# Decode attention with a gated FFN: K and V loaded head by head into adjacent partitions, FFN weights moved in the queue, a new tail

## The chip, the cores and the metric

One NeuronCore of a Trainium2 chip. The metric is device time in microseconds, the median of several executions. "Span" is the length of the profiled execution on the core, about 2 us less than its device time. A run is called slow here if it lies more than 1.5% above the fastest run of its kernel; ratios use the others ("fast") only.

PE is the matrix engine, DVE, ACT and POOL are the vector, scalar and general-purpose engines, and SP issues most of the loads; a "q" behind a name is its instruction queue. SBUF is the on-chip memory that loads fill, in 128 rows called partitions; products go to PSUM. FFN is the feed-forward network. The page is the printed summary of one profiled execution. A load is called landed at the last increment of its semaphore in the trace (16 increments for one load of K or V).

## The reference, cut to what matters

One decode step for two batches: layer norm, attention of 16 query heads over 8 K/V heads in a window of the last 2048 positions, then a gate from a small FFN.

```python
B, D = 2, 448; Hq, Hkv, Sk, Dh = 16, 8, 8192, 256; W = 2048; Dff = 1792
xn = layernorm(x)
q = xn @ wq                                      # wq: 448 x 4096
p = softmax(q . k_cache[:, :, Sk-W:, :] / 16)    # K, V: 2 x 8 x 8192 x 256, bf16
s = (p . v_cache[:, :, Sk-W:, :]) @ wo           # wo: 4096 x 448
g = silu(relu(xn @ w1) @ w2)                     # w1: 448 x 1792, w2: 1792 x 448
out = x + s * g
```

Each byte of the windows of K and V (33.6 MB), of wq and wo (3.7 MB each), and of w1 and w2 (1.6 MB each) is read once: 44.1 MB. Hardly anything is computed per byte.

## The kernel before

K and V are cut into four units of four heads, 4 MB for each of K and V. One unit's K goes through: transposes on PE, copies out of PSUM, scores, softmax. Its V is then multiplied. Loads are issued by the SP queue, in the order K0, wq, K1, V0, K2, V1, K3, V2, w1, w2, V3, wo, as buffers come free.

```python
def kv_src(u, cache):                    # partition = 4 * r + head, 32 KB of one head's rows each
    b, v = divmod(u, 2)
    return cache[b, 4*v:4*v+4, SK-W:SK, :].rearrange("h (r t) d -> r h (t d)", t=NT)   # NT = 64

def load_k(u):                           # one load of 128 partitions
    d_k[u] = pr.dma(SP, kbuf[u % 2][:, :], kv_src(u, A_k_cache), [st.get(("T", u - 2))])
# ... (cut)
# tail, after the softmax of unit 3:
do_H(); attend_turn(2); do_hT(); do_F(); do_PV(3); attend_scale(3); attend_turn(3)
# ... (cut: two products and two copies spread the attention output over partitions)
for j in range(32):                      # wo: four column groups of PE at once
    for i in range(4):
        lo = j * D + i * NCOL            # NCOL = 112
        m_o = pr.op(PE, mm(obk[32*i:32*i+B, 0:NCOL], at2[:, 2*j:2*j+2], wo_sb[:, lo:lo+NCOL],
                           j == 0, j == 31, tile_position=(0, 32*i)), deps)
# ... (cut) out = wo result * g + x, then one output DMA per batch, from SP and from ACT
```

Of the kernel before, what the change touches and what calls it, by code (L numbers as in the profile page):

```python
# [14 lines left out]
class _Op:  # L15
    __slots__ = ("eng", "fn", "deps", "dma", "needed", "value", "sem")

    def __init__(self, eng, fn, deps, dma):
        self.eng, self.fn, self.deps, self.dma = eng, fn, deps, dma
        self.needed, self.value, self.sem = dma, 0, None  # L20


class _Prog:
# [11 lines left out]
    def dma(self, eng, dst, src, deps=()):  # L35
        o = _Op(eng, lambda e: e.dma_start(dst, src), [d for d in deps if d is not None], True)  # L36
        self.lists[eng].append(o)
        return o

    def run(self, block):  # L40
        n = 0
# [4 lines left out]
        for e, ops in self.lists.items():  # L46
            sem, count = self.es.enter_context(self.nc.semaphore(f"s_{e}")), 0
            for o in ops:
                if o.dma:
                    n += 1  # L50
                    o.sem, o.value = self.es.enter_context(self.nc.semaphore(f"d_{n}")), 16
                elif o.needed:
                    count += 1
                    o.sem, o.value = sem, count

        def emit(eng, ops):
            seen = {}
            for o in ops:
# [9 lines left out]
                if o.needed:  # L68
                    made.then_inc(o.sem, 16 if o.dma else 1)
# [7 lines left out]
def bass_recurrent_scan__sliding_block_cached__dense_activation_relu__decode_kernel(  # L77
# [28 lines left out]
    WO_PARTS = [12, 12, 4, 2, 2]  # L106
    NCOL = D // 4
    NTB = 5
# [5 lines left out]
    with es:  # L114
# [17 lines left out]
        qmask = named("qmask", [128, 4], F32)  # L132
        own = named("own", [128, 4], F32)
        far = named("far", [128, 4], F32)
        low = named("low", [128, 4], F32)
        fold = named("fold", [128, 32], BF)
        fold8 = named("fold8", [128, 8], F32)
# [11 lines left out]
        h_sb = named("h_sb", [128, 28], BF)  # L149
        x_c = named("x_c", [128, NCOL], BF)  # L150
        ea = named("ea", [128, NCOL], F32)
        g_sb = named("g_sb", [128, NCOL], F32)
        tmp = named("tmp", [128, NCOL], F32)
        out_sb = named("out_sb", [128, NCOL], BF)
# [12 lines left out]
        at_exp = named("at_exp", [128, 256], BF)  # L167
        at2 = named("at2", [128, 64], BF)
# [13 lines left out]
        def kv_src(u, cache):  # L182
            b, v = divmod(u, 2)
            return cache[b, 4 * v:4 * v + 4, SK - W:SK, :].rearrange("h (r t) d -> r h (t d)", t=NT)

        d_x = pr.dma(ACTE, x_sb[0:B, :], A_x[:, 0, :])
        p_xc = pr.op(POOL, lambda e: e.memset(x_c[:, :], 0.0))
        d_xc = [pr.dma(ACTE, view(x_c, 0, [[1, NCOL]], n=4, p0=b, pstep=32),
                       A_x[b, 0, :].rearrange("(i n) -> i n", i=4), [p_xc]) for b in range(B)]

        wq_sb, w1_sb, w2_sb, wo_sb = vbuf[1], kbuf[0], kbuf[0], kbuf[1]
# [4 lines left out]
        wo_src = A_wo.rearrange("(p j) n -> p (j n)", j=32)  # L196
# [4 lines left out]
        def load_k(u):  # L201
            d_k[u] = pr.dma(SP, kbuf[u % 2][:, :], kv_src(u, A_k_cache), [st.get(("T", u - 2))])

        def load_v(u, cuts=(0, NT)):
            deps = [None if u == 0 else st["q_mm"] if u == 1 else st["PV", u - 2]]
            d_v[u] = []
            for lo, hi in zip(cuts, cuts[1:]):
                d_v[u].append((hi, pr.dma(SP, vbuf[u % 2][:, lo * DH:hi * DH],
                                          kv_src(u, A_v_cache)[:, :, lo * DH:hi * DH], deps)))
# [4 lines left out]
        load_v(0)  # L214

# [9 lines left out]
        p_qz = pr.op(POOL, lambda e: e.memset(qz[:, :], 0.0), [p_one])  # L225

# [9 lines left out]
        for e2 in range(2):  # L236
# [10 lines left out]
            out=qmask[:, :], in_=view(ident, 0, [[32, 4], [1, 32]]), axis=AX.X, op=ALU.add))  # L247

        def fold_op(e):
            with nc.allow_low_precision("zeros and ones"):  # L250
                return e.tensor_reduce(out=fold[:, :], in_=view(ident, 0, [[1, 32], [32, 4]]), axis=AX.X, op=ALU.add)
        v_fold = pr.op(DVE, fold_op)
        v_f8 = pr.op(DVE, lambda e: e.tensor_reduce(
# [5 lines left out]
        v_low = pr.op(DVE, lambda e: e.tensor_scalar(  # L259
            out=low[:, :], in0=own[:, :], scalar1=1.0, scalar2=-LOW, op0=ALU.subtract, op1=ALU.mult), [v_own])  # L260
# [49 lines left out]
        def softmax(u, fill=()):  # L310
            fill = list(fill)

            def meanwhile():
# [5 lines left out]
                out=rm4[:, :], in_=view(sbk, 0, [[1, 4], [4, 128]]), axis=AX.X, op=ALU.max), [st["S", u]])  # L319
# [16 lines left out]
                out=view(s_sb, 0, [[4, 128], [1, 4]]), in0=view(sbk, 0, [[4, 128], [1, 4]]), scalar=bias[:, 0:1],  # L336
                in1=view(low, 0, [[0, 128], [1, 4]]), op0=ALU.add, op1=ALU.min),
# [19 lines left out]

        def do_PV(u, gs=range(4)):
            bank, src, p = obk, vbuf[u % 2], pt[u % 2]
            for g in gs:  # L360
                deps = [next(d for hi, d in d_v[u] if hi >= 16 * g + 16), st["pt", u], a_z, st["obk"]]
# [9 lines left out]
        def attend_scale(u):  # L371
            st["osb", u] = st["obk"] = pr.op(DVE, lambda e: e.tensor_scalar(  # L372
                out=o_sb[:, :], in0=obk[:, :], scalar1=rs[:, u:u + 1], scalar2=None, op0=ALU.mult),
                [st["PV", u], st["rs", u], st.get(("oT", u - 1))])

        def attend_turn(u):
            b, v = divmod(u, 2)
            deps = [st["osb", u], v_fold, st["mbk"]]
            for dhi in range(2):
# [6 lines left out]
                out=view(at_exp, 128 * b + 64 * v, [[8, 8], [4, 2], [1, 4]]),  # L386
                in0=view(mbk, 136, [[1, 8], [8, 2], [0, 4]]),
                in1=view(qmask, 0, [[0, 8], [0, 2], [1, 4]]), op=ALU.mult), [o, v_qm])
# [35 lines left out]
        def do_hT():  # L424
            hbk = tb[0][:, :].bitcast(F32).tensor
            deps = [st["h_n"], evac[NU * NCHUNK - 4]]
            for j in range(7):
# [4 lines left out]
            st["hT"] = pr.op(DVE, lambda e: e.tensor_copy(  # L432
                view(h_sb, 0, [[2, 7], [14, 2], [1, 2]]), view(hbk, 0, [[4, 7], [2, 2], [1, 2]])), [o])

        def do_F():
            fbk = tb[1][:, :].bitcast(F32).tensor
            deps = [st["w2"], st["hT"], evac[NU * NCHUNK - 3]]
            for f in range(14):
                for i in range(4):
                    lo = W2_AT + f * D + i * NCOL  # L440
                    o = pr.op(PE, mm(view(fbk, 0, [[1, NCOL]], n=B, p0=32 * i), h_sb[:, 2 * f:2 * f + 2], w2_sb[:, lo:lo + NCOL],
# [109 lines left out]
```

## Time and profile before

| | before |
|---|---|
| device time, median | 112.91 us (112.71 to 113.01) |
| span | 110.9 us |
| read from HBM | 44.1 MB |
| landing of one 4 MB unit after the other (last engine of K1 to last of V2, 5 units) | 9.75 us |
| one 32 KB packet, median | 1213 ns |
| last landing of wo; end | 107.46; 110.9 us |

Packet times and landings of single engines come from the trace's packet and semaphore records. Lines from the page of the kernel before: busy tenths of the 16 DMA engines in 40 slices; the DMA queue (packets, MB, share of 16 engines' time); what was read; and the chain of work that ended last, by engine and by line.

```profile
span 110.9 us, 1921 instructions
...
DMA  3988979898899889889989998998999999999920
...
q1 hardware_dynamic: 2584, 44.11, 93.5%
...
HBM read 44.11 MB, written 0.00 MB: 398 GB/s over the span
...
DMA 56%; PE 34%; DVE 4%; SPq 2%; issue 1%; ACT 1%
```

Those engines are busy nearly everywhere. In this table of one stretch of the kernel before, the last two figures are the DMA share and GB/s:

```profile
core 0: us, PE busy (x) PEld busy (x) DVE busy (x) ACT busy (x) POOL busy (x), PEclk, DMA share, GB/s
30.00:70.00 40.00, 33.59 (x285) 22.04 (x284) 20.91 (x43) 15.90 (x20) 0.00 (x0) 0.83 1.00 431
```

At 431 GB/s, 44.1 MB take 102.3 us. The DMA issues of the kernel before (count, KB of one, median us from issue to landing) show one DMA per unit:

```profile
kbuf<-in_A_k_cache_dram SPq DMA_DIRECT2D x4, 4096.0 KB, 27.1
vbuf<-in_A_v_cache_dram SPq DMA_DIRECT2D x3, 4096.0 KB, 37.0
...
out_dram<-out_sb SPq DMA_DIRECT2D x1, 0.9 KB
out_dram<-out_sb ACTq DMA_DIRECT2D x1, 0.9 KB
```

And how often PE waits for K (total us, times, longest), and the end of the chain of waits (start, us, what):

```profile
PE tb L285 <- DMA kbuf<-in_A_k_cache_dram: 6.3, 2, 5.4
```

```profile
83.07 24.39 DMA kbuf<-in_A_wo_dram
107.46 0.04 issue
107.50 0.39 PE obk L265 x8
107.91 0.28 DVE tmp L513
108.22 0.27 DVE out_sb L515
```

The kernel ends when the last slice of wo has landed, plus 3.4 us. It is bound by the DMA stream.

### The profile page before, as it was taken

The page shows a single profiled execution, that of the slowest core. Times are in us where ns is not written, and L with a number is a line of the kernel's source. Part 1 is how long each engine was busy: PE and PEld are TensorE (multiplying, and loading weights), DVE is VectorE, ACT ScalarE, POOL GpSimd, SP SyncE. Part 2 cuts the span into 40 slices and gives each one's busy share as a digit, 9 for nine tenths or more (in the row PEclk, how much of TensorE's full clock was granted, in tenths as well). Part 3 has the DMA queues.
Part 4 walks back from the last instruction along what each step waited for, and adds up shares of the span by engine and source line. Part 5 has one row for each costly group of instructions (what it writes and reads, how often), then busy time and mean ns, then how long its engine had stood idle before and what let it go on. Part 6 is the DMA issues. An engine that isn't in the chain of part 4 may idle for free.

```text
span 110.9 us, 1921 instructions
## 1 busy us (share of the span) xinstructions
PE 74.0 (67%) x845; PEld 49.7 (45%) x845; DVE 48.0 (43%) x110; ACT 35.4 (32%) x43; POOL 1.9 (2%) x11
## 2 busy tenths in 40 slices
PE   0010299995428999859999949699985464293480
PEld 0000299952127977413777513397632244022350
DVE  2182042953433356553775653477546333104001
ACT  1960036760020647602286602076820200000000
POOL 6000000000000000000000000000000000000000
PEclk9999999999995589995899995799999985555555
DMA  3988979898899889889989998998999999999920
GB/s 95 473 379 379 520 331 496 355 567 372 378 532 414 378 378 556 384 378 532 417 366 390 526 402 378 520 426 378 387 382 416 454 434 423 408 426 427 394 98 1
DMA packets 2619, 44.22 MB, mean 399 GB/s; under 512 B 306, under 2 KB 564, under 8 KB 948
## 3 DMA queue, kind: packets, MB, share of 16 engines
q1 hardware_dynamic: 2584, 44.11, 93.5%
q8 instruction: 6, 0.10, 0.3%
q10 hardware_dynamic: 28, 0.00, 0.0%
q14 instruction: 1, 0.01, 0.0%
HBM read 44.11 MB, written 0.00 MB: 398 GB/s over the span
## 4 chain that ended last, share of the span: by engine, by line
DMA 56%; PE 34%; DVE 4%; SPq 2%; issue 1%; ACT 1%
DMA kbuf<-in_A_k_cache_dram 34%; PE tb L285 25%; DMA kbuf<-in_A_wo_dram 22%; PE sbk L265 5%; PE obk L265 2%; SPq L36 2%; PE mbk L265 1%; DVE s_sb L335 1%; ACT e_sb L340 1%; DVE rm L318 1%; DVE q_n L399 1%; PE mbk L345 1%; DVE pt L350 0%; DVE qz L409 0%; PE mbk L403 0%
## 5 line engine op out<-in xcount | busy, mean ns | idle before, releaser
L285 PE MATMUL tb<-ident_f,kbuf 128*128 128x128 f32 x256 | 36.6, 306 | 6.3 <-DMA kbuf<-in_A_k_cache_dram 6.3
L285 PEld LDWEIGHTS tb<-ident_f,kbuf 128*128 128x128 f32 x256 | 33.5, 161 | 10.4 <-DMA kbuf<-in_A_k_cache_dram 6.4
L295 ACT ACTIVATE kt<-tb 128x1024 bf16<-128x1024 bf16 x28 | 27.4, 1023 | 26.2 <-PE tb L285 26.2
L293 DVE COPY kt<-tb 128x1024 bf16<-128x1024 bf16 x36 | 24.7, 690 | 21.7 <-PE tb L285 21.7
L265 PE MATMUL obk<-vbuf,pt 128*16 128x512 bf16 x128 | 13.5, 529 | 3.5 <-DMA vbuf<-in_A_v_cache_dram 3.5
L265 PE MATMUL sbk<-kt,qz 128*32 128x512 bf16 x128 | 11.0, 393 | 1.7 <-DVE kt L293 1.1
L340 ACT ACTIVATE e_sb<-s_sb 128x512 bf16<-128x512 f32 x4 | 2.5, 630 | 22.9 <-DVE s_sb L335 22.9
L265 PEld LDWEIGHTS obk<-vbuf,pt 128*16 128x16 bf16 x128 | 3.2, 101 | 8.2 <-DMA vbuf<-in_A_v_cache_dram 4.4
L265 PE MATMUL mbk<-ident,xg 2*128 2x2 bf16 x7 | 0.3, 163 | 7.4 <-DVE xg L237 7.4
L372 DVE TENSOR_SCALAR o_sb<-obk,rs 128x512 bf16<-128x512 f32 x4 | 2.9, 735 | 5.4 <-PE obk L265 5.4
L265 PEld LDWEIGHTS sbk<-kt,qz 128*32 128x32 bf16 x128 | 2.7, 94 | 5.5 <-DVE kt L293 2.1
L265 PE MATMUL obk<-kbuf,at 128*2 128x112 bf16 x128 | 3.7, 292 | 2.1 <-DMA kbuf<-in_A_wo_dram 1.8
L318 DVE TENSOR_REDUCE rm<-sbk 128x4 f32<-128x512 f32 x4 | 2.8, 691 | 4.3 <-PE sbk L265 4.3
L350 DVE COPY pt<-mbk 128x512 bf16<-128x512 bf16 x4 | 1.7, 424 | 5.6 <-PE mbk L345 5.6
L345 PE MATMUL mbk<-ident,e_sb 128*128 128x128 bf16 x16 | 2.2, 286 | 2.6 <-ACT e_sb L340 2.6
L265 PEld LDWEIGHTS obk<-kbuf,at 128*2 128x2 bf16 x128 | 2.6, 112 | 3.1 <-DMA kbuf<-in_A_wo_dram 2.6
L265 PEld LDWEIGHTS mbk<-ident,xg 2*128 2x128 bf16 x7 | 0.3, 101 | 7.4 <-DVE xg L237 7.4
L345 PEld LDWEIGHTS mbk<-ident,e_sb 128*128 128x128 bf16 x16 | 1.3, 122 | 5.0 <-ACT e_sb L340 5.0
L323 PE MATMUL mbk<-ident_f,rm 128*1 128x128 f32 x4 | 1.1, 270 | 3.4 <-DVE rm L321 3.4
L265 PE MATMUL mbk<-one_f,mall 1*128 1x1 f32 x8 | 1.6, 268 | 2.5 <-DVE mall L330 2.5
L335 DVE SCALAR_TENSOR_TENSOR s_sb<-sbk,bias,low 128x512 f32<-128x512 f32 x4 | 3.0, 751 | 0.1
L323 PEld LDWEIGHTS mbk<-ident_f,rm 128*1 128x1 f32 x4 | 0.3, 79 | 5.4 <-DVE rm L321 5.4
(68 smaller groups left out, 37.0 us busy)
## 6 DMA issues: line engine op xcount, KB each, us to landing
kbuf<-in_A_k_cache_dram SPq DMA_DIRECT2D x4, 4096.0 KB, 27.1
vbuf<-in_A_v_cache_dram SPq DMA_DIRECT2D x3, 4096.0 KB, 37.0
vbuf<-in_A_wq_dram SPq DMA_DIRECT2D x1, 3584.0 KB, 20.1
kbuf<-in_B_w_dram SPq DMA_DIRECT2D x2, 1568.0 KB, 23.6
vbuf<-in_A_v_cache_dram SPq DMA_DIRECT2D x1, 3072.0 KB, 25.8
kbuf<-in_A_wo_dram SPq DMA_DIRECT2D x2, 1344.0 KB, 22.2
vbuf<-in_A_v_cache_dram SPq DMA_DIRECT2D x1, 1024.0 KB, 27.7
kbuf<-in_A_wo_dram SPq DMA_DIRECT2D x1, 448.0 KB, 24.3
```

The lines of the kernel that those rows point to most:

```text
L36: o = _Op(eng, lambda e: e.dma_start(dst, src), [d for d in deps if d is not None], True)
L265: return lambda e: e.matmul(out_ap, lhsT=lhsT, rhs=rhs, start=start, stop=stop, skip_group_check=True, **kw)
L285: o = pr.op(PE, lambda e, n=n, lo=lo: e.matmul(bank_f[:, n * 128:(n + 1) * 128], lhsT=src_f[:, lo:lo + 128], rhs=ident_f[:, :], start=True ...
L293: evac[n_th] = pr.op(DVE, lambda e: e.tensor_copy(dst[:, :], bank[:, :]), deps)
L295: evac[n_th] = pr.op(ACTE, lambda e: e.activation(dst[:, :], bank[:, :], ACT.Copy), deps)
L318: v = pr.op(DVE, lambda e: e.tensor_reduce(out=rm4[:, :], in_=view(sbk, 0, [[1, 4], [4, 128]]), axis=AX.X, op=ALU.max), [st["S", u]])
L323: m = st["rmT", u] = pr.op(PE, lambda e: e.matmul(mbk_ap(0, 128, 1), lhsT=rm[:, :], rhs=ident_f[:, :], start=True, stop=True, is_transpose ...
L335: v = st["shift", u] = pr.op(DVE, lambda e: e.scalar_tensor_tensor(out=view(s_sb, 0, [[4, 128], [1, 4]]), in0=view(sbk, 0, [[4, 128], [1, ...
L340: a = st["exp", u] = pr.op(ACTE, lambda e: e.activation(e_sb[:, :], s_sb[:, :], ACT.Exp, accum_out=ssum[:, 0:1]), [v, st.get(("Pt", u - 1) ...
L345: o = pr.op(PE, lambda e, j=j: e.matmul(mb16[:, 512 + 128 * j:640 + 128 * j], lhsT=e_sb[:, 128 * j:128 * j + 128], rhs=ident[:, :], start= ...
L350: v = st["pt", u] = pr.op(DVE, lambda e: e.tensor_copy(view(pt[u % 2], 0, [[256, 2], [16, 16], [8, 2], [1, 8]]), view(mb16, 512, [[256, 2] ...
L372: st["osb", u] = st["obk"] = pr.op(DVE, lambda e: e.tensor_scalar(out=o_sb[:, :], in0=obk[:, :], scalar1=rs[:, u:u + 1], scalar2=None, op0 ...
```

## The change

Its parts: each head of a unit gets its own plain load into 32 adjacent partitions (four loads per unit); w1 and w2 move up in the queue to between V0 and K2, into their own buffer, and the FFN is computed there; wo is read in two halves by head group, into K2's buffer, so that it no longer waits for K3; the wo and FFN products place each of the eight output rows (batch and quarter of the columns) in adjacent partitions, by shifted zero-padded weights, so that one output DMA does; a few idle products (`idle_work` in the code) are added on PE; I took them to be there for the PE clock, which the code does not say.

```diff
-            return cache[b, 4 * v:4 * v + 4, SK - W:SK, :].rearrange("h (r t) d -> r h (t d)", t=NT)
+            return cache[b, 4 * v:4 * v + 4, SK - W:SK, :].rearrange("h (r t) d -> h r (t d)", t=NT)
+
+        def kv_pairs(u, cache, buf, lo=0, hi=UW):
+            src = kv_src(u, cache)
+            return [(buf[32 * h:32 * h + 32, lo:hi], src[h, :, lo:hi]) for h in range(4)]
...
-            d_k[u] = pr.dma(SP, kbuf[u % 2][:, :], kv_src(u, A_k_cache), [st.get(("T", u - 2))])
+            d_k[u] = pr.dmas(SP, kv_pairs(u, A_k_cache, kbuf[u % 2]), [st.get(("T", u - 2))])
... (V alike; dmas issues a list of DMAs on one semaphore; the score masks follow the new partition order)
         load_v(0)
+        st["w1"] = pr.dma(SP, w1_sb[:, 0:W2_AT], w1_src)
+        st["w2"] = pr.dma(SP, ..., w2_src)
...
         attend_scale(0)
+        do_H()
+        do_hT()
+        do_F()
...
-    WO_PARTS = [12, 12, 4, 2, 2]
+    WO_PARTS = [8, 8, 6, 4, 4, 2]
-        wo_src = A_wo.rearrange("(p j) n -> p (j n)", j=32)
+        wo_src = A_wo.rearrange("(v p j) n -> v p (j n)", v=2, j=NWO)
...
-        do_H()
+        idle_work(3)
+        do_PV(3, (0,))
         attend_turn(2)
... (cut: the rest of unit 3's V products, spreads, idle products)
-                m_o = pr.op(PE, mm(obk[32 * i:32 * i + B, 0:NCOL], at2[:, 2 * j:2 * j + 2], wo_sb[:, lo:lo + NCOL],
-                                   j == 0, j == 31, tile_position=(0, 32 * i)), deps)
+                m_o = pr.op(PE, mm(obk[0:NROW, 0:NCOL], at_z[:, j * GAP + 3 - i:j * GAP + 3 - i + NROW],
+                                   wo_sb[:, lo:lo + NCOL], j == 0 and i == 0, j == 2 * NWO - 1 and i == 3), deps)
...
+        d_o = pr.dma(ACTE, out[:, 0, :].rearrange("b (i n) -> (b i) n", i=4), out_sb[:, :], [v_o])
```

More of the change, by code (lines that the diff above doesn't have):

```diff
@@ L19, in __init__ @@
         self.eng, self.fn, self.deps, self.dma = eng, fn, deps, dma
-        self.needed, self.value, self.sem = dma, 0, None
+        self.needed, self.value, self.sem = bool(dma), 0, None
 class _Prog:
@@ L35, in dma, with dmas @@
     def dma(self, eng, dst, src, deps=()):
-        o = _Op(eng, lambda e: e.dma_start(dst, src), [d for d in deps if d is not None], True)
+        return self.dmas(eng, [(dst, src)], deps)
+    def dmas(self, eng, pairs, deps=()):
+        o = _Op(eng, lambda e: [e.dma_start(dst, src) for dst, src in pairs], [d for d in deps if d is not None], len(pairs))
         self.lists[eng].append(o)
@@ L50, in run @@
                     n += 1
-                    o.sem, o.value = self.es.enter_context(self.nc.semaphore(f"d_{n}")), 16
+                    o.sem, o.value = self.es.enter_context(self.nc.semaphore(f"d_{n}")), 16 * o.dma
                 elif o.needed:
@@ L67, in emit @@
                 made = o.fn(eng) if o.fn else None
-                if o.needed:
-                    made.then_inc(o.sem, 16 if o.dma else 1)
+                if o.dma:
+                    for d in made:
+                        d.then_inc(o.sem, 16)
+                elif o.needed:
+                    made.then_inc(o.sem, 1)
         for name, e in (("gpsimd", POOL), ("sync", SP), ("scalar", ACTE), ("vector", DVE), ("tensor", PE)):
@@ L105, in bass_recurrent_scan__sliding_block_cached__dense_activation_relu__decode_kernel @@
     FC = DFF // 2
-    WO_PARTS = [12, 12, 4, 2, 2]
+    WO_PARTS = [8, 8, 6, 4, 4, 2]
+    NWO = 16
     NCOL = D // 4
+    NROW = 4 * B
+    GAP = NROW + 3
     NTB = 5
@@ L131, in bass_recurrent_scan__sliding_block_cached__dense_activation_relu__decode_kernel @@
         par2 = named("par2", [128, 2], F32)
-        qmask = named("qmask", [128, 4], F32)
+        qmask = named("qmask", [128, 8], F32)
         own = named("own", [128, 4], F32)
         far = named("far", [128, 4], F32)
-        low = named("low", [128, 4], F32)
+        low4 = named("low4", [128, 4], F32)
+        low = named("low", [128, 512], F32)
         fold = named("fold", [128, 32], BF)
+        fold16 = named("fold16", [128, NWO], BF)
         fold8 = named("fold8", [128, 8], F32)
@@ L148, in bass_recurrent_scan__sliding_block_cached__dense_activation_relu__decode_kernel @@
         h_n = named("h_n", [128, FC // 4], BF)
-        h_sb = named("h_sb", [128, 28], BF)
-        x_c = named("x_c", [128, NCOL], BF)
-        ea = named("ea", [128, NCOL], F32)
-        g_sb = named("g_sb", [128, NCOL], F32)
-        tmp = named("tmp", [128, NCOL], F32)
-        out_sb = named("out_sb", [128, NCOL], BF)
+        h_z = named("h_z", [128, 14 * GAP], BF)
+        x_c = named("x_c", [NROW, NCOL], BF)
+        ea = named("ea", [NROW, NCOL], F32)
+        g_sb = named("g_sb", [NROW, NCOL], F32)
+        tmp = named("tmp", [NROW, NCOL], F32)
+        out_sb = named("out_sb", [NROW, NCOL], BF)
         rm4 = named("rm4", [128, 4], F32)
@@ L166, in bass_recurrent_scan__sliding_block_cached__dense_activation_relu__decode_kernel @@
         o_sb = named("o_sb", [128, 512], BF)
-        at_exp = named("at_exp", [128, 256], BF)
-        at2 = named("at2", [128, 64], BF)
+        at_exp = named("at_exp", [128, 128], BF)
+        at_z = named("at_z", [128, 32 * GAP], BF)
+        wf = named("wf", [128, SLOTS * FC + 14 * D], BF)
         kbuf = [named(f"kbuf{i}", [128, UW], BF) for i in range(2)]
@@ L183, in kv_src @@
             b, v = divmod(u, 2)
-            return cache[b, 4 * v:4 * v + 4, SK - W:SK, :].rearrange("h (r t) d -> r h (t d)", t=NT)
+            return cache[b, 4 * v:4 * v + 4, SK - W:SK, :].rearrange("h (r t) d -> h r (t d)", t=NT)
+        def kv_pairs(u, cache, buf, lo=0, hi=UW):
+            src = kv_src(u, cache)
+            return [(buf[32 * h:32 * h + 32, lo:hi], src[h, :, lo:hi]) for h in range(4)]
         d_x = pr.dma(ACTE, x_sb[0:B, :], A_x[:, 0, :])
-        p_xc = pr.op(POOL, lambda e: e.memset(x_c[:, :], 0.0))
-        d_xc = [pr.dma(ACTE, view(x_c, 0, [[1, NCOL]], n=4, p0=b, pstep=32),
-                       A_x[b, 0, :].rearrange("(i n) -> i n", i=4), [p_xc]) for b in range(B)]
-        wq_sb, w1_sb, w2_sb, wo_sb = vbuf[1], kbuf[0], kbuf[0], kbuf[1]
+        d_xc = pr.dma(ACTE, x_c[:, :], A_x[:, 0, :].rearrange("b (i n) -> (b i) n", i=4))
+        wq_sb, w1_sb, w2_sb, wo_sb = vbuf[1], wf, wf, kbuf[0]
         W2_AT = SLOTS * FC
@@ L207, in load_v @@
             for lo, hi in zip(cuts, cuts[1:]):
-                d_v[u].append((hi, pr.dma(SP, vbuf[u % 2][:, lo * DH:hi * DH],
-                                          kv_src(u, A_v_cache)[:, :, lo * DH:hi * DH], deps)))
+                d_v[u].append((hi, pr.dmas(SP, kv_pairs(u, A_v_cache, vbuf[u % 2], lo * DH, hi * DH), deps)))
         load_k(0)
@@ L214, in bass_recurrent_scan__sliding_block_cached__dense_activation_relu__decode_kernel @@
         load_v(0)
+        st["w1"] = pr.dma(SP, w1_sb[:, 0:W2_AT], w1_src)
+        st["w2"] = pr.dma(SP, w2_sb[:, W2_AT:W2_AT + 14 * D].rearrange("p (hf f) -> p hf f", hf=2), w2_src)
         i0 = pr.op(POOL, lambda e: e.memset(ident[:, :], 0.0))
@@ L225, in bass_recurrent_scan__sliding_block_cached__dense_activation_relu__decode_kernel @@
         p_qz = pr.op(POOL, lambda e: e.memset(qz[:, :], 0.0), [p_one])
+        p_z = [pr.op(POOL, lambda e, t=t: e.memset(t[:, :], 0.0)) for t in (h_z, at_z)][-1]
         a_z = [pr.op(ACTE, lambda e, t=t: e.memzero(t[:, :])) for t in (obk,)][-1]
@@ L246, in bass_recurrent_scan__sliding_block_cached__dense_activation_relu__decode_kernel @@
         v_qm = pr.op(DVE, lambda e: e.tensor_reduce(
-            out=qmask[:, :], in_=view(ident, 0, [[32, 4], [1, 32]]), axis=AX.X, op=ALU.add))
+            out=qmask[:, :], in_=view(ident, 0, [[16, 8], [1, 16]]), axis=AX.X, op=ALU.add))
         def fold_op(e):
@@ L252, in bass_recurrent_scan__sliding_block_cached__dense_activation_relu__decode_kernel, with fold16_op @@
         v_fold = pr.op(DVE, fold_op)
+        def fold16_op(e):
+            with nc.allow_low_precision("zeros and ones"):
+                return e.tensor_reduce(out=fold16[:, :], in_=view(ident, 0, [[1, NWO], [NWO, 8]]), axis=AX.X, op=ALU.add)
+        v_fold16 = pr.op(DVE, fold16_op)
         v_f8 = pr.op(DVE, lambda e: e.tensor_reduce(
@@ L258, in bass_recurrent_scan__sliding_block_cached__dense_activation_relu__decode_kernel @@
             out=far[:, :], in0=own[:, :], scalar1=1.0, scalar2=-FAR, op0=ALU.subtract, op1=ALU.mult), [v_own])
-        v_low = pr.op(DVE, lambda e: e.tensor_scalar(
-            out=low[:, :], in0=own[:, :], scalar1=1.0, scalar2=-LOW, op0=ALU.subtract, op1=ALU.mult), [v_own])
+        v_low4 = pr.op(DVE, lambda e: e.tensor_scalar(
+            out=low4[:, :], in0=own[:, :], scalar1=1.0, scalar2=-LOW, op0=ALU.subtract, op1=ALU.mult), [v_own])
+        v_low = pr.op(DVE, lambda e: e.tensor_copy(
+            view(low, 0, [[128, 4], [32, 4], [1, 32]]), view(low4, 0, [[0, 4], [1, 4], [0, 32]])), [v_low4])
         v_gs = pr.op(DVE, lambda e: e.tensor_copy(
@@ L318, in softmax @@
             v = pr.op(DVE, lambda e: e.tensor_reduce(
-                out=rm4[:, :], in_=view(sbk, 0, [[1, 4], [4, 128]]), axis=AX.X, op=ALU.max), [st["S", u]])
+                out=rm4[:, :], in_=view(sbk, 0, [[32, 4], [128, 4], [1, 32]]), axis=AX.XY, op=ALU.max), [st["S", u]])
             v = pr.op(DVE, lambda e: e.tensor_tensor(out=rmm[:, :], in0=rm4[:, :], in1=far[:, :], op=ALU.add), [v, v_far])
@@ L335, in softmax @@
             v = st["shift", u] = pr.op(DVE, lambda e: e.scalar_tensor_tensor(
-                out=view(s_sb, 0, [[4, 128], [1, 4]]), in0=view(sbk, 0, [[4, 128], [1, 4]]), scalar=bias[:, 0:1],
-                in1=view(low, 0, [[0, 128], [1, 4]]), op0=ALU.add, op1=ALU.min),
+                out=s_sb[:, :], in0=sbk[:, :], scalar=bias[:, 0:1], in1=low[:, :], op0=ALU.add, op1=ALU.min),
                 [v, v_low, st.get(("exp", u - 1))])
@@ L356, in softmax, with out_bank @@
             assert not fill
+        obk_last = tb[3][:, :].bitcast(F32).tensor
+        def out_bank(u):
+            return obk if u < NU - 1 else obk_last
         def do_PV(u, gs=range(4)):
-            bank, src, p = obk, vbuf[u % 2], pt[u % 2]
+            bank, src, p = out_bank(u), vbuf[u % 2], pt[u % 2]
             for g in gs:
-                deps = [next(d for hi, d in d_v[u] if hi >= 16 * g + 16), st["pt", u], a_z, st["obk"]]
+                deps = [next(d for hi, d in d_v[u] if hi >= 16 * g + 16), st["pt", u], a_z if u < NU - 1 else st["tb3"], st["obk"]]
                 for a in range(2):
@@ L371, in attend_scale @@
         def attend_scale(u):
-            st["osb", u] = st["obk"] = pr.op(DVE, lambda e: e.tensor_scalar(
-                out=o_sb[:, :], in0=obk[:, :], scalar1=rs[:, u:u + 1], scalar2=None, op0=ALU.mult),
+            v = st["osb", u] = pr.op(DVE, lambda e: e.tensor_scalar(
+                out=o_sb[:, :], in0=view(out_bank(u), 0, [[1, 512]]), scalar1=rs[:, u:u + 1], scalar2=None, op0=ALU.mult),
                 [st["PV", u], st["rs", u], st.get(("oT", u - 1))])
+            if u < NU - 1:
+                st["obk"] = v
         def attend_turn(u):
-            b, v = divmod(u, 2)
             deps = [st["osb", u], v_fold, st["mbk"]]
@@ L385, in attend_turn, with attend_spread @@
             st["at", u] = st["mbk"] = pr.op(DVE, lambda e: e.tensor_tensor(
-                out=view(at_exp, 128 * b + 64 * v, [[8, 8], [4, 2], [1, 4]]),
-                in0=view(mbk, 136, [[1, 8], [8, 2], [0, 4]]),
-                in1=view(qmask, 0, [[0, 8], [0, 2], [1, 4]]), op=ALU.mult), [o, v_qm])
+                out=view(at_exp, 0, [[16, 8], [8, 2], [1, 8]]),
+                in0=view(mbk, 136, [[1, 8], [8, 2], [0, 8]]),
+                in1=view(qmask, 0, [[0, 8], [0, 2], [1, 8]]), op=ALU.mult), [o, v_qm, st.get(("m_at", u - 1))])
+        def attend_spread(u):
+            b, v = divmod(u, 2)
+            o = st["m_at", u] = pr.op(PE, mm(mbk_ap(256, NWO), at_exp[:, :], fold16[:, :], True, True),
+                                      [st["at", u], v_fold16, st["mbk"]])
+            st["at_z", v] = st["mbk"] = pr.op(DVE, lambda e: e.tensor_copy(
+                view(at_z, NWO * GAP * v + 3 + 4 * b, [[GAP, NWO]]), mbk_ap(256, NWO)), [o, p_z])
         def do_q():
@@ L425, in do_hT @@
             hbk = tb[0][:, :].bitcast(F32).tensor
-            deps = [st["h_n"], evac[NU * NCHUNK - 4]]
+            deps = [st["h_n"], evac[2 * NCHUNK - 2]]
             for j in range(7):
@@ L431, in do_hT @@
                     deps = []
-            st["hT"] = pr.op(DVE, lambda e: e.tensor_copy(
-                view(h_sb, 0, [[2, 7], [14, 2], [1, 2]]), view(hbk, 0, [[4, 7], [2, 2], [1, 2]])), [o])
+            st["hT"] = evac[2 * NCHUNK - 2] = pr.op(DVE, lambda e: e.tensor_copy(
+                view(h_z, 3, [[GAP, 7], [7 * GAP, 2], [4, 2]]), view(hbk, 0, [[4, 7], [2, 2], [1, 2]])), [o, p_z])
         def do_F():
             fbk = tb[1][:, :].bitcast(F32).tensor
-            deps = [st["w2"], st["hT"], evac[NU * NCHUNK - 3]]
+            deps = [st["w2"], st["hT"], evac[2 * NCHUNK - 1]]
             for f in range(14):
@@ L440, in do_F @@
                     lo = W2_AT + f * D + i * NCOL
-                    o = pr.op(PE, mm(view(fbk, 0, [[1, NCOL]], n=B, p0=32 * i), h_sb[:, 2 * f:2 * f + 2], w2_sb[:, lo:lo + NCOL],
-                                     f == 0, f == 13, tile_position=(0, 32 * i)), deps)
+                    o = pr.op(PE, mm(view(fbk, 0, [[1, NCOL]], n=NROW), h_z[:, f * GAP + 3 - i:f * GAP + 3 - i + NROW],
+                                     w2_sb[:, lo:lo + NCOL], f == 0 and i == 0, f == 13 and i == 3), deps)
                     deps = []
-            f_ap = view(fbk, 0, [[1, NCOL]])
+            st["F"] = o
+            f_ap = view(fbk, 0, [[1, NCOL]], n=NROW)
             a_e = pr.op(ACTE, lambda e: e.activation(ea[:, :], f_ap, ACT.Exp, scale=-1.0), [o])
@@ L448, in do_F, with idle_work @@
             v_rc = pr.op(DVE, lambda e: e.reciprocal(tmp[:, :], ea[:, :]), [v_d])
-            st["g"] = pr.op(DVE, lambda e: e.tensor_tensor(
+            st["g"] = evac[2 * NCHUNK - 1] = pr.op(DVE, lambda e: e.tensor_tensor(
                 out=g_sb[:, :], in0=f_ap, in1=tmp[:, :], op=ALU.mult), [v_rc])
+        def idle_work(n):
+            wbk = tb[2][:, :].bitcast(F32).tensor
+            deps = [evac[NU * NCHUNK - 2], v_fold]
+            for _ in range(n):
+                pr.op(PE, mm(view(wbk, 0, [[1, 512]]), ident[:, :], kt[0][:, 0:512], True, True), deps)
+                deps = []
         def scores(u):
@@ L458, in scores @@
                     attend_turn(u - 2)
+                if i == 5 and u > 1:
+                    attend_spread(u - 2)
             do_S(u, 3)
@@ L475, in bass_recurrent_scan__sliding_block_cached__dense_activation_relu__decode_kernel @@
         attend_scale(0)
+        do_H()
+        do_hT()
+        do_F()
         load_v(2)
         scores(2)
-        st["w1"] = pr.dma(SP, w1_sb[:, 0:W2_AT], w1_src, [st["T", 2]])
-        st["w2"] = pr.dma(SP, w2_sb[:, W2_AT:W2_AT + 14 * D].rearrange("p (hf f) -> p hf f", hf=2), w2_src,
-                          [st["T", 2]])
         softmax(2, values(1))
@@ L483, in bass_recurrent_scan__sliding_block_cached__dense_activation_relu__decode_kernel @@
         load_v(3, (0, 48, 64))
-        scores(3)
-        d_wo = []
-        j0 = 0
-        for n in WO_PARTS:
-            d_wo.append((j0, pr.dma(SP, wo_sb[:, j0 * D:(j0 + n) * D], wo_src[:, j0 * D:(j0 + n) * D], [st["T", 3]])))
-            j0 += n
+        d_wo, j0 = {}, 0
+        for n in WO_PARTS:
+            v, j = divmod(j0, NWO)
+            d_wo[j0] = pr.dma(SP, wo_sb[:, j0 * D:(j0 + n) * D], wo_src[v, :, j * D:(j + n) * D], [st["T", 2]])
+            j0 += n
+        scores(3)
+        st["tb3"] = pr.op(ACTE, lambda e: e.memzero(tb[3][:, :]), [evac[NU * NCHUNK - 1]])
@@ L490, in bass_recurrent_scan__sliding_block_cached__dense_activation_relu__decode_kernel @@
         softmax(3, values(2))
         attend_scale(2)
-        do_H()
+        idle_work(3)
+        do_PV(3, (0,))
         attend_turn(2)
-        do_hT()
-        do_F()
-        do_PV(3)
+        do_PV(3, (1,))
+        attend_spread(2)
+        do_PV(3, (2, 3))
         attend_scale(3)
+        idle_work(3)
         attend_turn(3)
-        for b in range(2):
-            m_at = pr.op(PE, mm(mbk_ap(256 + 32 * b, 32), at_exp[:, 128 * b:128 * b + 128],
-                                fold[:, :], True, True), [st["at", NU - 1], v_fold, st["mbk"]])
-            v_at2 = st["mbk"] = pr.op(DVE, lambda e, b=b: e.tensor_copy(
-                view(at2, b, [[2, 32]]), mbk_ap(256 + 32 * b, 32)), [m_at])
@@ L504, in bass_recurrent_scan__sliding_block_cached__dense_activation_relu__decode_kernel @@
-        deps = [v_at2, st["obk"]]
-        landed = dict(d_wo)
-        for j in range(32):
-            deps = deps + [landed.get(j)]
+        idle_work(1)
+        attend_spread(3)
+        deps = [st["obk"]]
+        for j in range(2 * NWO):
+            deps = deps + [d_wo.get(j), st["at_z", j // NWO]]
             for i in range(4):
                 lo = j * D + i * NCOL
-                m_o = pr.op(PE, mm(obk[32 * i:32 * i + B, 0:NCOL], at2[:, 2 * j:2 * j + 2], wo_sb[:, lo:lo + NCOL],
-                                   j == 0, j == 31, tile_position=(0, 32 * i)), deps)
+                m_o = pr.op(PE, mm(obk[0:NROW, 0:NCOL], at_z[:, j * GAP + 3 - i:j * GAP + 3 - i + NROW],
+                                   wo_sb[:, lo:lo + NCOL], j == 0 and i == 0, j == 2 * NWO - 1 and i == 3), deps)
@@ L512, in bass_recurrent_scan__sliding_block_cached__dense_activation_relu__decode_kernel @@
                 deps = []
         v_t = pr.op(DVE, lambda e: e.tensor_tensor(
-            out=tmp[:, :], in0=obk[:, 0:NCOL], in1=g_sb[:, :], op=ALU.mult), [m_o, st["g"]])
+            out=tmp[:, :], in0=obk[0:NROW, 0:NCOL], in1=g_sb[:, :], op=ALU.mult), [m_o, st["g"]])
         v_o = pr.op(DVE, lambda e: e.tensor_tensor(
-            out=out_sb[:, :], in0=tmp[:, :], in1=x_c[:, :], op=ALU.add), [v_t, *d_xc])
-        d_o = [pr.dma((SP, ACTE)[b], out[b, 0, :].rearrange("(i n) -> i n", i=4),
-                      view(out_sb, 0, [[1, NCOL]], n=4, p0=b, pstep=32), [v_o]) for b in range(B)]
@@ L519, in bass_recurrent_scan__sliding_block_cached__dense_activation_relu__decode_kernel @@
-        pr.op(SP, None, d_o)
+            out=out_sb[:, :], in0=tmp[:, :], in1=x_c[:, :], op=ALU.add), [v_t, d_xc])
+        d_o = pr.dma(ACTE, out[:, 0, :].rearrange("b (i n) -> (b i) n", i=4), out_sb[:, :], [v_o])
+        pr.op(ACTE, None, [d_o])
         with nc.Block() as block:
```

## The prediction

> **What bounds it now.** The DMA engines. The DMA queues view shows 44.1 MB in a span of 110.9 us, the engines busy in nearly every slice up to 107 us. Successive 4 MB loads land 9.72 us apart (431 GB/s), and a 32 KB packet takes 1213 ns (27 GB/s per engine), early and late. The chain of waits ends in DMA wo (22%), 8 matmuls, output. Three things add to about 102 us of transfer: a start of about 3 us (K0 is issued at 0.74 and lands at 13.0, though it needs 9.7; half of the engines start their first packet at 2.16 us, half at 2.87, all end it near 4.15), 1.5 us of skew at the end (ten engines finish at 105.9, six at 107.4; each of the six lost 1.45 us once, near an instruction-fetch packet), and a tail of 3.4 us after the last wo landing at 107.46 (matmuls 0.4, DVE 0.6, output 2.4).
>
> **What the change does.**
> 1. Bytes stay 44.1 MB, packets of K and V 32 KB. Four issues per load cost SP about 0.6 us each, against 2.4 us that 1 MB takes: hidden. Smaller first DMAs may start all engines together: estimate -0.3 us.
> 2. w1, w2 before K2 only reorders bytes. K2, V1, K3, V2 land 7.3 us later (estimate: 3.2 MB at 431 GB/s), V3 and wo where they did. K3 lands near 79, its transposes and scores take 9.6 us, its softmax about 6: unit 3's weights are ready near 95, just ahead of V3 (96.3). H and F (4 us) leave the end, where the wait for V3 already hid them.
> 3. wo no longer waits for K3, but it was issued 19 us before it landed anyway: 0.
> 4. Tail: one spread instead of two, so wo matmuls begin near 101.2 instead of 102.4. But they no longer run in four column groups at once (27 ns each at half clock now). [...] No such matmul here. wo's transfer takes 8.7 us[...]
> 5. Output by one DMA instead of two, which landed 0.36 us apart: -0.3 us.
>
> **Sum:** 112.9 - 0.3 + 0.3 - 0.3, about 112.6; allowing for tuning: **112.3 us**, range 110.6 to 113.8. Chances: faster by over 2% 0.14, within 2% 0.72, slower 0.14.
>
> **What would show it.** K landings 9.7 us apart; K2 near 59; DMA busy to 107; first packets closer together; granted clock 1.0 at wo; [...] one output DMA.
>
> **What would make it wrong.** [...] Every large load of this trace covers 128 partitions, so it can't tell. [...] K and V take twice as long and the time is near 190 us; I give it 0.1, since idle work and a finely cut wo make sense only beside full-rate loads. Also: [...] a start that gains more than 1 us.

The sum came to 112.9 - 0.3 (point 1) + 0.3 (point 4) - 0.3 (point 5), about 112.6, and to 112.3 with the allowance for tuning. The term +0.3 was worked out from a pace for wo products one after another; the -0.3 of point 1 is an estimate of mine beside the measured starts (2.16 and 2.87 us). In the last paragraph, what is given 0.1 is that loads of 32 partitions run at half the rate of loads of 128.

## The result, and the profile after

| | before | after |
|---|---|---|
| device time, median | 112.91 us | 196.88 us (195.95 to 197.65) |
| span | 110.9 us | 195.9 us |
| landing of one 4 MB unit after the other | 9.75 us | 20.06 us (K2 to V2, 3 units) |
| one 32 KB packet, median | 1213 ns | 2564 ns |
| last landing of wo; end | 107.46; 110.9 us | 191.22; 195.9 us |

The ratio is 1.744 (95% interval 1.734 to 1.753): 74% slower. A ratio is the mean time of one kernel's fast runs over that of the other's of the same rounds, so it is not quite the ratio of the medians quoted.

The page of the changed kernel, the same lines:

```profile
span 195.9 us, 1971 instructions
...
DMA  9998899999999889999999999999999899999960
...
q1 hardware_dynamic: 3152, 44.11, 96.1%
...
HBM read 44.11 MB, written 0.00 MB: 225 GB/s over the span
...
DMA 49%; PE 29%; another core or an unknown queue 15%; SPq 2%; DVE 2%; issue 1%
```

The 15% under "another core or an unknown queue" are four waits for loads too: each ends within 0.05 us of the landing of V0, K2, V1 or the last part of V3. The end of the changed kernel's chain of waits (start, us, what):

```profile
180.39 2.25 another core or an unknown queue
182.69 2.42 PE tb L288 x9
185.19 0.45 PE tb L288
185.78 7.86 PE obk L288 x128
```

The 128 wo products, now one after another, end at 193.6 us, 2.4 us after the last landing of wo.

The same bytes, and engines that are even busier: 96% instead of 93%. Busy here means that a packet is under way, not how fast its bytes move. In a stretch of the changed kernel that holds only K and V:

```profile
core 0: us, PE busy (x) PEld busy (x) DVE busy (x) ACT busy (x) POOL busy (x), PEclk, DMA share, GB/s
102.00:162.00 60.00, 31.79 (x243) 22.20 (x243) 18.05 (x35) 15.20 (x17) 0.00 (x0) 0.67 0.99 207
```

The DMA issues, and PE's wait for K, of the changed kernel:

```profile
kbuf<-in_A_k_cache_dram SPq DMA_DIRECT2D x16, 1024.0 KB, 51.5
vbuf<-in_A_v_cache_dram SPq DMA_DIRECT2D x12, 1024.0 KB, 72.6
...
out_dram<-out_sb ACTq DMA_DIRECT2D x1, 1.8 KB
```

```profile
PE tb L308 <- DMA kbuf<-in_A_k_cache_dram: 53.5, 4, 16.3
```

K and V are slow, and wq is not: it still fills 128 partitions with one load, and lands 8.9 us after K0, at (3.67 MB / 8.87 us) 414 GB/s. (w2, the load just before K2, landed 5.6 us after w1, against 3.8 in the kernel before.) All 16 engines take part in each short load: the first sixteen packets start between 1.74 and 2.46 us, and each load's semaphore receives 16 separate increments.

Where the 85.0 us of span went: eight units (four of K, four of V) times 10.31 us (20.06 - 9.75) make 82.5. From the last wo landing to the end there are 4.6 us instead of 3.4, which is 1.2. The last 1.3 us are not assigned; the later landing of w2 may be among them.

### The profile page after: what moved, and what is told of

Read it like the earlier page. It is cut to its first block, busy times and chain, and to the rows that moved or that the text cites. A ratio compares the mean times of both kernels' runs of the same rounds, so it can differ in the third digit from the quotient of the medians.

```text
span 195.9 us, 1971 instructions
## 1 busy us (share of the span) xinstructions
PE 93.1 (48%) x854; PEld 63.7 (33%) x854; DVE 49.9 (25%) x114; ACT 36.2 (19%) x44; POOL 2.3 (1%) x12
## 3 DMA queue, kind: packets, MB, share of 16 engines
q1 hardware_dynamic: 3152, 44.11, 96.1%
## 4 chain that ended last, share of the span: by engine, by line
DMA 49%; PE 29%; another core or an unknown queue 15%; SPq 2%; DVE 2%; issue 1%
DMA kbuf<-in_A_k_cache_dram 25%; DMA vbuf<-in_A_v_cache_dram 24%; PE tb L308 10%; PE obk L288 8%; PE tb L288 6%; SPq L39 2%; PE sbk L288 2%; PE mbk L288 1%; DVE kt L316 1%; PE mbk L367 1%; DVE o_sb L399 0%; PE mbk L346 0%; DVE mrow L349 0%; DVE mall L353 0%
## 5 line engine op out<-in xcount | busy, mean ns | idle before, releaser
L308 PE MATMUL tb<-ident_f,kbuf 128*128 128x128 f32 x256 | 41.4, 331 | 53.5 <-DMA kbuf<-in_A_k_cache_dram 53.5
L308 PEld LDWEIGHTS tb<-ident_f,kbuf 128*128 128x128 f32 x256 | 37.4, 174 | 58.0 <-DMA kbuf<-in_A_k_cache_dram 53.9
L288 PE MATMUL obk<-vbuf,pt 128*16 128x512 bf16 x96 | 11.8, 619 | 20.0 <-DMA vbuf<-in_A_v_cache_dram 20.0
L288 PEld LDWEIGHTS obk<-vbuf,pt 128*16 128x16 bf16 x96 | 1.9, 100 | 23.9 <-DMA vbuf<-in_A_v_cache_dram 21.5
L288 PE MATMUL tb<-vbuf,pt 128*16 128x512 bf16 x32 | 4.1, 614 | 10.1 <-DMA vbuf<-in_A_v_cache_dram 10.1
L288 PE MATMUL obk<-kbuf,at_z 128*8 128x112 bf16 x128 | 7.9, 235 | 0.0
L288 PEld LDWEIGHTS obk<-kbuf,at_z 128*8 128x8 bf16 x128 | 7.7, 99 | 0.0
L288 PE MATMUL tb<-wf,h_z 128*8 128x112 bf16 x56 | 4.5, 266 | 0.5 <-DVE h_z L467 0.5
L288 PEld LDWEIGHTS tb<-wf,h_z 128*8 128x8 bf16 x56 | 4.3, 113 | 0.5 <-issue 0.5
L413 DVE TENSOR_TENSOR at_exp<-mbk,qmask 128x128 bf16<-128x128 f32 x4 | 1.2, 290 | 10.1 <-PE mbk L288 10.1
```

Source lines behind the costliest of these rows:

```text
L288: return lambda e: e.matmul(out_ap, lhsT=lhsT, rhs=rhs, start=start, stop=stop, skip_group_check=True, **kw)
L308: o = pr.op(PE, lambda e, n=n, lo=lo: e.matmul(bank_f[:, n * 128:(n + 1) * 128], lhsT=src_f[:, lo:lo + 128], rhs=ident_f[:, :], start=True ...
L413: st["at", u] = st["mbk"] = pr.op(DVE, lambda e: e.tensor_tensor(out=view(at_exp, 0, [[16, 8], [8, 2], [1, 8]]), in0=view(mbk, 136, [[1, 8 ...
```

## The experiments

Theory A: the four loads of 32 adjacent partitions are the whole cause, because of which partitions the load in progress fills, whatever its source and the number of loads (A1; the ground for its figures by pattern, 216 and 108 GB/s, no trace had shown). Rivals within A: many short loads are slow (A2), or one head at a time is a slow source (A3). Theory B: the new order or the tail is a large part of it.

### The loads put back

In the changed kernel, only the loads and the score masks that belong to them are as before.

```diff
-            return [(buf[32 * h:32 * h + 32, lo:hi], src[h, :, lo:hi]) for h in range(4)]
+            return [(buf[:, lo:hi], kv_src(u, cache)[:, :, lo:hi])]        # "r h (t d)" again
```

> The changed kernel with only the K and V loads put back: one load of 128 partitions per unit (partition 4r + head), with the score masks that go with it; FFN early, wo in halves, output in eight partitions all stay. Theory A (the four loads of 32 adjacent partitions are the whole cause): the time comes back to that of before, 111.5 to 114 us, K and V landings 9.7 us apart. Theory B (the new order or the tail is a large part of the cause): at least 125 us. Within A the rest of the change is worth -1.5 to +1 us.

Measured: correct, 114.03 us (112.65 to 114.64, six runs, two of them slow), ratio to before 1.006 (1.002 to 1.010). The 74% are gone. The rest of the change costs 0.6%; it does not help. (The fastest of the six, 112.65, is what makes two of them slow by the rule; all six together average 0.9% above before.)

### The loads alone

In the kernel before, only the loads and their masks are as after.

> The kernel before with only the K and V loads changed to four loads of 32 adjacent partitions per unit, and the score masks that go with it. Theory A: nearly all of the loss is here, 185 to 200 us, a 32 KB packet near 2565 ns as in the changed kernel instead of 1213. Theory B: under 150 us.

Measured: correct, 196.41 us, ratio 1.745 (1.742 to 1.748); a 32 KB packet 2565 ns. The part alone makes the whole loss. Theory B falls.

### The pattern by itself

Eight stages in one program, each 3.1 MB from the K cache into SBUF with 24 KB per partition, each after the one before has landed. Its output is wrong, which doesn't matter for the time. It ran once, so a stage's spread from run to run is not known.

```python
stage((SP, [(b128[:, :], rows(0, 0, 4))]))                                                # 1
stage((SP, [(part(b32, 32 * h, 32), heads(0, 4 + h, 1)[0]) for h in range(4)]))            # 2
stage((SP, [(part(b64, 64 * g, 64), rows(1, 2 * g, 2)) for g in range(2)]))                # 3
stage((SP, [(part(bstep, h, 32, 4), heads(1, 4 + h, 1)[0]) for h in range(4)]))            # 4: h, h + 4, ...
stage((SP, [... 8 loads of 16 adjacent partitions ...]))                                   # 5
stage((SP, [... heads 0, 1 as in stage 2 ...]), (ACTE, [... heads 2, 3 ...]))              # 6
stage((SP, [... 4 loads of 128 partitions, a quarter of each row ...]))                    # 7
stage((SP, [(bk4[:, :], heads(1, 4, 4))]))                                                 # 8: source "h r (t d)"
```

> Not the function (wrong result on purpose): eight stages, each loads 3.1 MB from the K cache, the next stage only after it landed; only the pattern differs. Theory A1 [...]: one load of 128 partitions 430 GB/s while streaming; 4 loads of 32 adjacent partitions and 2 loads of 64 adjacent ones both 216; 8 loads of 16 adjacent ones 108; 4 loads of every fourth partition, with the same source and count as the 4 adjacent ones, well above 216, up to 430; 4 loads of 128 partitions with a quarter of each row 430. Theory A2 (many or short loads, or two packets per engine, are slow): every fourth partition as slow as 32 adjacent, 64 adjacent faster than 32. Theory A3 (a source of one head at a time, one contiguous MB of HBM, is slow): every fourth partition as slow as 32 adjacent, 64 adjacent (two heads) faster. Heads 0, 1 from one queue and 2, 3 from another at once: A1 between 216 (if they go one after the other) and 430 (if the engines alternate). One load with the heads outermost in its source: 4 engines only, 108 GB/s, which would be why four loads were written.

One stretch per stage, from its first packet's start to its last packet's end, in the order of the stages (last figure: GB/s, start and drain included):

```profile
core 0: us, POOL busy (x), PEclk, DMA share, GB/s
3.53:11.78 8.25, 0.00 (x0) 1.00 0.91 381
13.14:28.61 15.47, 0.00 (x0) 1.00 0.97 203
30.79:46.02 15.23, 0.00 (x0) 1.00 0.96 205
48.15:56.93 8.78, 0.00 (x0) 1.00 0.88 356
58.24:85.11 26.87, 0.00 (x0) 1.00 0.98 116
87.27:101.64 14.37, 0.00 (x0) 1.00 0.96 219
103.87:113.37 9.50, 0.00 (x0) 1.00 0.96 331
115.11:171.02 55.91, 0.00 (x0) 1.00 0.24 56
```

| stage | destination of one load | 24 KB packet, median |
|---|---|---|
| 1 | 128 partitions | 912 ns |
| 2 | 32 adjacent | 1924 ns |
| 3 | 64 adjacent | 1931 ns |
| 4 | 32, every fourth | 912 ns |
| 5 | 16 adjacent | 3382 ns |
| 6 | 32 adjacent, two queues | 1742 ns |

Stages 2 and 4 differ in nothing but which partitions a load fills (and which batch it reads), and are 1924 and 912 ns: A2 and A3 fall. Stage 3, twice the partitions of stage 2 in one load, gains nothing (1931 ns, 205 GB/s against 203). Stage 5, 16 adjacent partitions, is nearly halved again (116 GB/s). That is what A1 expected, though the 116 of stage 5 lie above its 108. The runs show which partitions make a load slow; why it is these is not shown. Two queues (stage 6) give 8% more than one (219 to 203): they do not merge the halves. In stage 7, 6 KB packets take 234 ns in the median, nearly the rate of stage 1 (4 times 234 is 936), but a tenth took 344 or more and the stage made 331 GB/s against 381: short loads of full width cost some of the rate, not half of it.

Stage 8 is the one DMA that would have kept the partition order 32 * head + r. It used 4 engines: its semaphore was incremented five times in all, once at the start and once by each engine, and the DMA share of the 16 engines was 0.24. My 108 GB/s for it, four times 27, was a miss: it made 56. Why it took 4 engines, and why they made only about half of that, is not shown.

### Every fourth partition

In the changed kernel, only the destination partitions of the four loads (and the masks) differ.

```diff
-            return [(buf[32 * h:32 * h + 32, lo:hi], src[h, :, lo:hi]) for h in range(4)]
+            return [(view(buf, lo, [[1, hi - lo]], n=32, p0=h, pstep=4), src[h, :, lo:hi]) for h in range(4)]
```

> The changed kernel with one thing altered: each of the four loads of a unit goes to every fourth partition (head, head + 4, ...) instead of 32 adjacent ones, with the score masks for that. Source, number, size and order of the loads stay. Theory A1 [...]: 112 to 116 us, like the run with the loads put back. Theories A2, A3 (many short loads, or one head at a time as source): 185 us or more.

Measured: correct, 113.80 us (113.52 to 114.22), ratio 1.009 (1.007 to 1.011). Middle of its stream:

```profile
core 0: us, PE busy (x) PEld busy (x) DVE busy (x) ACT busy (x) POOL busy (x), PEclk, DMA share, GB/s
30.00:70.00 40.00, 33.56 (x346) 25.34 (x347) 18.46 (x37) 15.00 (x19) 0.00 (x0) 0.79 1.01 429
```

Same count, size, source and order of the loads as in the changed kernel, and 429 GB/s instead of 207 (434 from 60 to 89 us, where this kernel too moves only K and V). This is the cause, in place.

This run also shows, in a fast profile, what the rest of the change does at the end. Its timeline (start, us, engine, line, operation), idle products, first V3 products, wo products and output:

```profile
96.58 1.44 PE L288 MATMUL tb<-kt,ident 128*128 128x512 bf16 x3
...
97.95 1.03 PE L288 MATMUL tb<-vbuf,pt 128*16 128x512 bf16 x8
...
103.34 6.46 PE L288 MATMUL obk<-kbuf,at_z 128*8 128x112 bf16 x128
...
110.42 0.30 ACTq L39 DMA_DIRECT2D out_dram<-out_sb  x1
```

K3 landed at 79.4 us and V3's first part at 96.4, but its products begin at 97.95, behind the sums and the scaling of unit 2 and the idle products. The wo products start at 103.34 and end 2.0 us after the last landing (107.8): the core no longer waits for the stream at the end.

### What the rest of the change is worth

All ratios from here on are inside 2%; the text goes by their intervals.

Starting from the loads put back, w1 and w2 go back to between V2 and V3, and the FFN to the end. The three idle products before V3's products are dropped with that; four later ones stay.

```diff
         load_v(0)
-        st["w1"] = ...; st["w2"] = ...
...
         load_v(2)
+        st["w1"] = ...; st["w2"] = ...
...
         attend_scale(2)
-        idle_work(3)
-        do_PV(3, (0,))
+        do_H()
         attend_turn(2)
+        do_hT()
+        do_F()
+        do_PV(3, (0,))
```

> The run with the loads put back, and also w1, w2 loaded between V2 and V3 again and the FFN at the end again, as in the kernel before; own buffer, wo in halves and the eight output rows stay. Theory C (that run ends late because K3, V1, V2 land 7.3 us later, so the computation after K3 and not the DMA ends last): K3 lands near 71.6, wo waits for its own landings, 112.0 to 113.2 us. Theory D (it ends late because the wo products no longer run in four column groups): as long as that run, 113.5 to 114.5 us.

Measured: correct, 112.63 us (112.56 to 113.61), ratio 1.000 (0.997 to 1.003); K3 landed at 71.75 us. Theory D, as stated, falls: with the same kind of wo products the 0.6% are gone. Two of the six runs still took 113.6, the profiled one among them: its granted clock was 0.5 from 67.6 to 77.8 us, while K3's transposes ran, and the wo products started at 103.07 and ended 1.8 us after the last landing (107.69). In the next run, with K3 landed at the same time, it was 0.5 only from 66.7 to 70.1, and they started at 101.50. So a part of the spread may be the clock; no run tests it.

The same without the idle products:

```diff
         attend_scale(3)
-        idle_work(3)
         attend_turn(3)
-        idle_work(1)
         attend_spread(3)
```

> The same without the idle products. If they are what raises the clock for wo: granted clock 0.5 there, [...] 113.5 to 116 us. If the FFN and the products of V3 keep the clock up by themselves: no difference over 0.5 us.

Measured: correct, 112.63 us (112.56 to 113.21), ratio 0.999 (0.998 to 1.001). The clock records of its profile give full clock from 97.4 us, before wo starts at 101.5. In this order idle products are not needed. No run took them out of the changed order.

The opposite test, in the kernel before: only w1, w2 moved up, into their own buffer.

```diff
         load_v(0)
+        st["w1"] = pr.dma(SP, w1_sb[:, 0:W2_AT], w1_src)
+        st["w2"] = pr.dma(SP, ..., w2_src)
...
-        st["w1"] = pr.dma(..., [st["T", 2]])
-        st["w2"] = pr.dma(..., [st["T", 2]])
```

> The kernel before with only the place of w1, w2 in the queue changed (after V0, into their own buffer; the FFN stays at the end, wo stays in four column groups). Theory C: K3 lands near 79 instead of 71.6, the chain of work after K3 ends last, the FFN now stands in it, 113.5 to 115 us. If the place of these 3.2 MB does not matter: 112.5 to 113.2 us.

Measured: correct, 115.52 us (113.51 to 115.89; two of four runs slow, so the ratio rests on two), ratio 1.013 (1.007 to 1.019). Three of the four lie between 115.2 and 115.9; the profiled one, 115.21, just counts as fast. Its chain of waits (start, us, what):

```profile
44.25 35.26 DMA kbuf<-in_A_k_cache_dram
79.55 1.97 PE tb L288 x16
...
97.70 1.50 PE obk L268 x28
...
100.60 1.47 PE tb L268 x56
102.08 3.29 PE obk L268 x32
105.39 0.76 DVE o_sb L375
...
107.73 2.57 PE obk L268 x128
110.33 0.29 DVE tmp L513
```

The chain no longer passes through wo's transfer. K3 lands at 79.5 us instead of 71.6, its transposes begin at 79.55, the FFN (97.70 to about 102) and V3's products follow, and all 128 wo products start at 107.73, when the last wo slice has landed too (107.71). Theory C holds: 3.2 MB ahead of K3 cost time though the total of bytes is the same, because 16 us of work on K3 must be done before V3 is of use, and the wait for V3 that used to hide the FFN (3.5 us on PE in the kernel before) is gone. How the 0.6 to 0.9% of the changed order divide between K3's later landing and its slower wo products (6.46 us for 128, against 2.57 in four column groups here) is not shown: no run had the early FFN with four column groups.

### Tries at a faster kernel

Four loads of every fourth partition, with the FFN late:

```diff
-            return [(buf[:, lo:hi], kv_src(u, cache)[:, :, lo:hi])]
+            src = kv_src(u, cache)                                     # "r h (t d)"
+            return [(view(buf, lo, [[1, hi - lo]], n=32, p0=h, pstep=4), src[:, h, lo:hi]) for h in range(4)]
```

> The run with the FFN late, with four loads of every fourth partition per unit. If the earlier start of the small first loads (first packets 1.74 to 2.46 us against 2.16 to 2.97) counts and the rate is kept: 0.3 to 0.5 us faster than the run with the FFN late. If every fourth partition costs rate (in the pattern run a tenth of the packets took 1061 ns instead of 912): 1 us or more slower.

Measured: correct, 112.70 us, ratio 1.000 (0.998 to 1.003). Neither expectation came: first packets started between 2.06 and 2.99 us, so the earlier start of the adjacent loads did not come over, and K0 landed at 13.2 (before: 13.1).

From the run with late FFN and no idle products: useful wo products where idle ones stood.

```diff
-    WO_PARTS = [8, 8, 6, 4, 4, 2]
+    WO_PARTS = [4, 4, 8, 6, 4, 4, 2]
...
+        do_wo(range(4), [st["at_z", 0], st["obk"]])
         attend_turn(3)
         attend_spread(3)
+        do_wo(range(4, NWO), [])
+        do_wo(range(NWO, 2 * NWO), [st["at_z", 1]])
```

> The run with the FFN late and no idle products, with the first four slices of wo cut small and multiplied while the last unit's output is scaled, so that wo's products start about 0.8 us earlier. Its single output DMA took 1.6 us from issue to the end against 2.4 with two. If wo's products are what ends last there: 112.0 to 112.4 us, 0.5% faster than before. If the DMA alone ends last: 112.6.

Measured: correct, 112.76 us (112.60 to 112.81), ratio 0.9986 (0.9974 to 0.9998): 0.1% faster than before, not 0.5%. In its profile V3's products ended only near 101.4, behind the FFN, and the wo products near 108.7, 1.0 us after the last landing at 107.71.

The same with w1, w2 between K3 and V2, and the FFN between unit 3's scores and its softmax:

```diff
         load_k(3)
+        st["w1"] = ...; st["w2"] = ...
...
         load_v(2)
-        st["w1"] = ...; st["w2"] = ...
...
+        do_H()
+        do_hT()
+        do_F()
         softmax(3, values(2))
         attend_scale(2)
-        do_H()
-        attend_turn(2)
-        do_hT()
-        do_F()
         do_PV(3, (0,))
+        attend_turn(2)
```

> The same with w1, w2 between K3 and V2 and the FFN between unit 3's scores and its softmax, so that neither K3 nor the products of V3 wait for it. If the FFN at the end still delayed the products of V3 (by about 1 us in that run): 0.2 to 0.6 us faster than the run before it in this call. If V2's later landing (about 89) holds up the last softmax: slower by up to 1 us.

Measured: correct, 112.72 us (112.54 to 114.05), ratio 1.0015 (0.998 to 1.005). No gain: the last softmax ended near 96.1 us, and V3's products still ended near 101.1. In all of these kernels the last slice of wo lands between 107.4 and 107.9 us. No version beats the kernel before by more than 0.1%, because none shortens the stream.

## Why the prediction was wrong

- What bounds the kernel: right. It was DMA-bound, and a change of rate in the stream is a change of the time.
- Point 1, "Four issues per load cost SP about 0.6 us each, against 2.4 us that 1 MB takes: hidden": the step that failed. The issue time was hidden, but 1 MB did not take 2.4 us. It took 5.0 (20.06 / 4). The 2.4 us were worked out from loads of 128 partitions and carried to loads of 32, a shape that the trace did not hold.
- The last paragraph named the right case and size ("K and V take twice as long and the time is near 190 us"; measured 196.9), and gave it 0.1. The reason given, that "idle work and a finely cut wo make sense only beside full-rate loads", judged the author of the change and not the machine. Nothing in the trace spoke for that reason; it held no large load of fewer than 128 partitions. The range left the case out.
- Point 2: K3 landing near 79 and unit 3's weights ready near 95 were right once loads of full rate were used (79.4 and 95.7 in the run with every fourth partition). What I left out is what stands between the weights and V3's products on PE: V3 could have been used at 96.4 and was at 97.95.
- Point 3: nothing in the runs speaks against it; wo was bound by its place in the stream.
- Point 4: measured, 128 wo products took 6.46 us, 50 ns each, at full clock in the run with every fourth partition. Their start was mis-sized: 103.3 instead of 101.2. That idle work is needed for the clock was not shown: with the FFN late, leaving it out changed nothing (112.63 us with and without).
- Point 5: the gain of one output DMA was mis-sized. From its issue to the end of the span it took 1.6 us (109.14 to 110.76, FFN late without idle work), two took 2.4 (108.52 to 110.88). Part of it went into the wo products, which ended 0.8 us after the last landing instead of 0.4.
- "A start that gains": first packets did start 0.4 us earlier, and it was lost in the halved rate.
- "1.5 us of skew at the end": in the kernel before, five engines each fell about 1.45 us behind and one about 1, in turn, each near an instruction packet (five of 16 KB, one of 8 KB); the prediction had 1.45 for all six. The last landing waits for the slowest engine (105.9 against 107.46 us). That these packets are the cause was tested by no run.

## What to carry to other kernels

Before splitting a load, ask which partitions each single DMA fills: 32 or 64 adjacent ones made 203 and 205 GB/s in the test, 16 made 116. Loads queued one behind another did not merge into a wide one (207 GB/s in the changed kernel). If a load must be split, give each part every fourth partition (429 GB/s in place, from loads of 1 MB, against 431 from loads of 4 MB), or split the free dimension (331 against 381 in the test). A DMA share of 99%, as in the changed kernel, says that packets are under way: divide bytes by time in the middle of the stream. And where the trace holds no load of the new shape, a guess about why someone wrote the code should not set the odds: measure that shape.
